# Unit 1 of the output projection in seven half-size products, with its weight sums earlier and batch 2's turns divided and moved

## The chip, the cores and the metric

One Trainium2 chip, one of its NeuronCores. The metric is the device time of one execution in microseconds (us). Five engines with a queue of instructions each work side by side: TensorE (PE in the profile; PEld is its weight load), VectorE (DVE), ScalarE (ACT), GpSimd (POOL) and SyncE (SP, which here only issues DMAs). They wait for each other through semaphores.

## The reference

Attention with a forget gate, then a two-layer network without a bias. With 8 batches, 8 heads, 576 positions and a head size of 64:

```python
scores = (q @ k.T) / 8 + cum[:, None] - cum[None, :]   # cum = cumsum(log(clip(f)))
scores = where(causal, -1e9, scores)
x = softmax(scores) @ v                                # 4608 tokens x 512, heads side by side
h = x @ w_in                                           # 512 -> 2048
g = h - tanh(h)
out = g @ w_out                                        # 2048 -> 512, float32
```

## The kernel before, in words

The attention is worked through in 32 **pairs** of heads, `(batch b, c)` with c from 0 to 3, and the network in nine **units** u of 512 tokens. The order on every engine is the order of the program text (a manual schedule), and the main loop is written as **slots** p = 4 to 32. Slot p (function `slot`, items from `att_items`) emits seven score tiles of pair p (`scores`, L342 on: matmuls L358 into two PSUM buffers, ScalarE's exponential L367, GpSimd's mask L377), the attention values of pair p-1 (`values`: 30 small matmuls L386, then three VectorE instructions L392 to L394 that divide by the row sum), and the turning of their result by two transposing DMAs on SP into the token ring XR (`turn`, L401 and L403). Between these items it emits steps of the network from one long list, `mlp`; `TAKE` says how many steps a slot takes, and they are spread evenly over the items that carry a name.

The network's first layer is `mlp1(u, s)`: four matmuls of 512 columns (L462; for unit 0 eight of 256, L448) into one of the three buffers of the PSUM pool `ps_m`, then `gate`: ScalarE's tanh (L414) and VectorE's sum of both (L415), which frees the buffer. The second layer has two forms.

- `mlp2(u, s)`, 16 steps for a unit: four matmuls of 512 columns each (L581), every fourth step an eviction by ScalarE (L585) and a store by SP (L587). Before the change units 0 and 1 use it.
- `seven(u, s)`, 14 steps for a unit: Strassen's scheme in Winograd's form, in which seven products of half size take the place of eight. Each step has eight matmuls of 256 columns (`product`, L503), into one running PSUM chain `cx` (from the one-buffer pool `ps_tr`) or a tile `cz` (from `ps_m`). ScalarE copies the chain out four times for a unit (`keep`, L540), VectorE adds four times (`add`, L496), SP stores four times (L493). It needs 16 sums of quarters of the unit's g (`sums`, L429, VectorE, 128x512), spread over the unit's steps by `mlp1` and `more_sums`. It also needs four sums of quarters of w_out, t1, t2, t3 and tn4, made once, in 16 VectorE instructions (`weight_sums`, L438). Units 2 to 8 use this form (`fast(u)`).

The weight sums lie in slots 11 to 14 (`LOADS`, L220). Of their results tn4 has a tile of its own; t1, t2 and t3 lie in the buffers `raw[0][1]` and `raw[1][1]`, which before that hold q and k of batch 1 and then of batch 3. Batch 3's are read out by one long transposing DMA for q (`turn_all` to TQ, slot 8) and one for k (to TK, slot 9), on SP.

For batches 1 and 2, q and k are turned by TensorE (`trans`, L245): six transposes (L254) into one PSUM tile, then two copies of 64x576 into QT or KT, one for the even and one for the odd columns (L260 to L266). Each copy is given to ScalarE (A, L261) or VectorE (V, L263) by a string of two letters: batch 1's q has "AV", batch 1's k and all of batch 2 have "VV". Slot p turns pair p+1: q at its score tile 0, k at tile 3 (in slot 7 at tiles 2 and 4). The PSUM tile comes from `ps_tr`, which has one buffer; k of batch 1 takes one from `ps_m`. Batch 2's q and k are loaded in slot 4 by GpSimd, in one DMA each (L214, L218).

Of the kernel before, what the change touches and what calls it, by code (L numbers as in the profile page):

```python
# [9 lines left out]
FP16 = mybir.dt.float16  # L10
# [7 lines left out]
FAR = 3  # L18
# [4 lines left out]
def kernel(  # L23
# [11 lines left out]
    P = 128  # L35

    B, H, S, D = q.shape
# [4 lines left out]
    NPAIR = H // 2  # L42
# [6 lines left out]
    NFT = DFF // P  # L49
# [3 lines left out]
    NU = NT // UW  # L53
# [3 lines left out]
    wpl = ctx.enter_context(tc.tile_pool(name="wpl", bufs=1))  # L57
# [11 lines left out]
    wout = wpl.tile([P, NFT, DM], FP16)  # L69
    HF, HD = NFT // 2, DM // 2  # L70
    SW = [wpl.tile([P, HF // 2, UW], FP16, tag=f"sw{i}", name=f"sw{i}") for i in range(2)]
    tn4 = wpl.tile([P, HF, HD], FP16, tag="tn4", name="tn4")
    RB = 3
    RING = RB * S
    XR = wpl.tile([P, NCH, RING], FP16)
# [5 lines left out]
    HP, LEAD = NJ * D, 2 * P  # L81
    TC = NPAIR * PITCH + LEAD
    TW = HF * HD
    tp = [raw[0][1][:, 0:TW], raw[1][1][:, 0:TW]]
    t2 = [raw[i][1][:, TW:TW + TW // 2].rearrange("p (k e) -> p k e", e=HD) for i in range(2)]
    t1, t3 = (x.rearrange("p (k e) -> p k e", e=HD) for x in tp)
    vn = [qkp.tile([P, NJ, H, VW], FP16, tag=f"vn{i}", name=f"vn{i}") for i in range(2)]
    QT = [qkp.tile([D + 3, H, S], FP16, tag=f"QT{i}", name=f"QT{i}") for i in range(2)]
    KT = [qkp.tile([D + 3, H, PITCH], FP16, tag=f"KT{i}", name=f"KT{i}") for i in range(2)]
# [12 lines left out]
    def load_heads(dst, src, b, n):  # L102
        pn = min(P, S - n * P)
        to = dst[0:pn, n * P:n * P + D]
        to = bass.AP(to.tensor, to.offset, [list(to.ap[0]), [HP, H], [1, D]])
        nc.gpsimd.dma_start(out=to, in_=src[b, :, n * P:n * P + pn, :].rearrange("h p d -> p h d"))  # L106

    def turn_all(dst, src):
        nc.sync.dma_start_transpose(out=dst.rearrange("p (x t) -> p x t", t=P), in_=src[:, 0:TC])
# [103 lines left out]
    def load_qk(dst, src, b, h0, h1):  # L213
        nc.gpsimd.dma_start(  # L214
            out=dst[b % 2][:, h0:h1, :, :].rearrange("p h n d -> p h (n d)"),
            in_=src[b, h0:h1, :, :].rearrange("h (p n) d -> p h (n d)", n=NT6))

    LOADS = {(NPAIR, 5): [lambda: load_qk(qn, q, 2, 0, H)],  # L218
             (NPAIR, 6): [lambda: load_qk(kn, k, 2, 0, H)]}
    for i in range(2 * HF):  # L220
        LOADS.setdefault((2 * NPAIR + 3 + i // 4, i % 4 * 2), []).append(lambda i=i: weight_sums(i))
    for b in range(2, B):
        p0 = (b - 1) * NPAIR
        for n in range(NJ):
            LOADS.setdefault((p0 + (2 if b == 2 else 1), n), []).append(lambda b=b, n=n: load_v(b, n))
        LOADS.setdefault((p0, 0), []).append(lambda b=b: load_aug(b))
        if b < FAR:
            continue
# [9 lines left out]
    E, XN, GT, M2, AV = {}, {}, {}, {}, {}  # L238
# [5 lines left out]

    def trans(b, c, src, dst, eng):  # L245
        pn, g3 = S // NT6, NT6 // 2
        if b == 1 and src is kn:
            t32 = ps_m.tile([P, UW], FP32, tag="m", name="t32")
        else:
            t32 = ps_tr.tile([P, UW], FP32, tag="tr", name="t32")  # L250
        t16 = t32.bitcast(FP16)[:, 0:2 * S // 2].rearrange("p (a g n) -> p a g n", a=2, g=g3)
        for a in range(2):
            for g in range(g3):
                nc.tensor.transpose(out=t16[:, a, g, :],  # L254
                                    in_=src[b % 2][:, 2 * c + a, 2 * g:2 * g + 2, :],
                                    identity=id16[0:pn, 0:pn])
        for e in range(2):
            to = dst[b % 2][0:D, 2 * c:2 * c + 2, e:S:2].rearrange("d a (p g) -> d a p g", g=g3)
            of = t16[e * D:(e + 1) * D, :, :, :].rearrange("d a g p -> d a p g")
            if eng[e] == "A":  # L260
                nc.scalar.activation(out=to, in_=of, func=AF.Copy)  # L261
            else:
                nc.vector.tensor_copy(out=to, in_=of)  # L263
# [134 lines left out]
    def turn(b, c):  # L398
        xn = XN.pop((b, c))
        r0 = b % RB * S  # L400
        nc.sync.dma_start_transpose(out=XR[:, c, r0:r0 + S - D].rearrange("p (n t) -> p n t", t=P),  # L401
                                    in_=xn[:, 0:NJ - 1, :].rearrange("p n d -> p (n d)"))
        nc.sync.dma_start_transpose(out=XR[:, c, r0 + S - D:r0 + S], in_=xn[D:P, NJ - 1, :])  # L403
# [11 lines left out]
        nc.vector.tensor_tensor(out=to, in0=view(hps), in1=view(th), op=ALU.add)  # L415

    def fast(u):
        return u > 1

    def quarter(u, k, hf, e):  # L420
        return G[(u, k)].rearrange("p (h e) n -> p h e n", h=2)[:, hf, e, :]
# [9 lines left out]
    def weight_sums(i):  # L431
        what, x = divmod(i, HF // 2)
        lo, hi = slice(2 * x, 2 * x + 2), slice(HF + 2 * x, HF + 2 * x + 2)
        b11, b12, b21, b22 = (wout[:, r, c] for r in (lo, hi) for c in (slice(0, HD), slice(HD, DM)))
        t2x = t2[x // 2][:, x % 2 * 2:x % 2 * 2 + 2, :]
        out, in0, in1 = ((t1[:, lo, :], b12, b11), (t2x, b22, t1[:, lo, :]),
                         (t3[:, lo, :], b22, b12), (tn4[:, lo, :], b21, t2x))[what]
        nc.vector.tensor_tensor(out=out, in0=in0, in1=in1, op=ALU.subtract)  # L438

    def mlp1(u, s):  # L440
# [43 lines left out]
    def moving(what, ft):  # L484
        if what[0] == "b":
            return wout[:, ft + HF * (what[1] == "2"), HD * (what[2] == "2"):HD * (what[2] == "2") + HD]
        if what == "t2":
            return t2[ft // 4][:, ft % 4, :]
        return {"t1": t1, "t3": t3, "tn4": tn4}[what][:, ft, :]
# [113 lines left out]

    FEW = {3: ("s1", "s4", "s6"), 4: ("s1", "s3", "s4", "s6")}

    def att_items(p):
# [3 lines left out]
        after = pairs[p + 1] if p + 1 < len(pairs) else None  # L610
        for ti in range(len(TILES)):
            if here:
                items.append((lambda ti=ti: scores(*here, ti), "s%d" % ti))
            for load in LOADS.get((p, ti), ()):
                items.append((load, ""))
            late = 2 * (p == 2 * NPAIR - 1)
            if ti == late and after and after[0] < FAR:
                items.append((lambda: trans(*after, qn, QT, "AV" if after[0] == 1 else "VV"), "q"))
            if ti == 1 and before:
                items.append((lambda: (values(*before), turn(*before)), "v"))  # L620
            if ti == 3 + late // 2 and after and after[0] < FAR:
                items.append((lambda: trans(*after, kn, KT, "VV"), "k"))
        return items

    goal = [0]
# [114 lines left out]
    scores0(4, 3)  # L740
    step()
    trans(1, 0, qn, QT, "AV")
    scores0(4, 4)
    turn0(3)
# [40 lines left out]
```

## Time and profile before

| | us |
|---|---|
| median of 3 runs | 345.33 (345.21 to 345.88) |
| the profiled execution | 346.0 |
| its span, first to last instruction | 344.3 |
| TensorE busy | 334.6 |
| VectorE busy | 236.2 |
| ScalarE busy | 222.9 |
| GpSimd busy | 158.6 |

The profile is of one execution; its own time is 0.67 us above the median and 1.7 us above its span. "Busy" on TensorE counts a matmul until its modelled end, so that it may be busy in the profile and still have waited; the way to find a wait is to lay out what a slot has to do and to compare that with the slot's length. A slot is counted here from the first of the 30 small matmuls of one pair's values (`av`) to the first of the next: slot 8's values begin at 65.58 us, slot 9's at 74.43, slot 10's at 85.33, slot 11's at 95.03.

### The profile page before, as it was taken

How to read it: one execution, taken by the hardware profiler on the slowest of the kernel's cores; microseconds unless marked ns; L12 is line 12 of the kernel's file. 1: busy time of each engine (PE TensorE's matmuls, PEld its weight loads, DVE VectorE, ACT ScalarE, POOL GpSimd, SP SyncE). 2: the span in 40 equal slices, each digit the busy share in tenths (PEclk: the TensorE clock that was granted, in tenths of full speed). 3: DMA queues.
4: the chain of work that ended last, by engine and by line, in shares of the span. 5: the costliest groups of instructions: out<-in, count | busy, mean ns of one | idle time of the engine just before them, and what ended most of it. 6: DMA issues, size and time to landing. Idle time of an engine off the chain costs nothing.

```text
span 344.3 us, 8688 instructions
## 1 busy us (share of the span) xinstructions
PE 334.6 (97%) x3354; PEld 235.2 (68%) x3354; DVE 236.2 (69%) x481; ACT 222.9 (65%) x417; POOL 158.6 (46%) x318
## 2 busy tenths in 40 slices
PE   7989999999999999999999999999999999999995
PEld 3879875655455557888886568656887786486485
DVE  6496886658953598558764895478637865975973
ACT  4677976558755786578757875687568844623631
POOL 8966448755267726664586548652222210000000
PEclk9999999999999999999999999999999999999999
DMA  9999999999799999999999999999330013002002
GB/s 88 140 197 188 204 203 141 169 159 233 126 141 127 202 175 151 123 193 184 164 145 188 172 159 181 182 172 184 91 110 19 17 50 109 3 30 93 0 32 91
DMA packets 161323, 45.96 MB, mean 134 GB/s; under 512 B 141506, under 2 KB 159234, under 8 KB 161282
## 3 DMA queue, kind: packets, MB, share of 16 engines
q0 software_dynamic: 100128, 18.36, 74.8%
q1 hardware_dynamic: 61074, 26.99, 39.8%
q8 instruction: 26, 0.43, 0.6%
q14 instruction: 15, 0.12, 0.1%
q10 hardware_dynamic: 80, 0.07, 0.1%
HBM read 36.85 MB, written 9.44 MB: 134 GB/s over the span
## 4 chain that ended last, share of the span: by engine, by line
PE 88%; DVE 5%; ACT 4%; POOL 1%; issue 1%; DMA 1%; ACTq 0%; DVEq 0%
PE hps L462 31%; PE cx L503 14%; PE cz L503 11%; PE ps L358 10%; PE ops L581 7%; PE av L386 7%; PE hps L448 2%; PE ps L300 2%; DVE gt L415 1%; PE t L272 1%; ACT e L305 1%; DVE QT L263 1%; ACT e L367 1%; ACT th L414 1%; PE av L313 1%
## 5 line engine op out<-in xcount | busy, mean ns | idle before, releaser
L415 DVE TENSOR_TENSOR gt<-hps,th 128x512 f16<-128x512 f32 x144 | 98.4, 688 | 42.7 <-ACT th L414 41.6
L462 PE MATMUL hps<-XR,win 128*128 128x512 f16 (+4 forms) x640 | 125.7, 336 | 0.2 <-DVE gt L415 0.2
L367 ACT ACTIVATE e<-ps 128x512 f16<-128x512 f32 x168 | 98.5, 594 | 37.4 <-PE ps L358 34.7
L414 ACT ACTIVATE th<-hps 128x512 f32<-128x512 f32 x144 | 86.1, 598 | 29.5 <-PE hps L462 19.8
L377 POOL TENSOR_SCALAR_AFFINE_SELECT e<-e 128x128 f16<-128x128 f16 x162 | 55.3, 342 | 105.9 <-ACT e L367 105.6
L462 PEld LDWEIGHTS <-win 128*128 128x128 f16 x640 | 56.3, 97 | 43.7 <-issue 0.5
L358 PE MATMUL ps<-QT,KT 67*128 67x512 f16 (+1 forms) x336 | 68.7, 277 | 0.5 <-DVE KT L263 0.3
L503 PEld LDWEIGHTS <-gt 128*128 128x128 f16 x560 | 52.5, 97 | 8.2 <-DVE gt L415 0.4
L358 PEld LDWEIGHTS <-KT 67*128 67x128 f16 x336 | 31.9, 98 | 21.7 <-DVE KT L263 0.8
L95 POOL DMA_DIRECT2D vn<-in_v_dram x40 | 34.2, 859 | 5.9 <-DMA win<-in_moe_w_in_dram 3.0
L581 PE MATMUL ops<-wout,gt 128*128 128x512 f16 x128 | 32.6, 378 | 0.0
L386 PEld LDWEIGHTS <-e 128*128 128x128 f16 x784 | 28.1, 97 | 3.3
L496 DVE TENSOR_TENSOR snap<-cz,snap 128x512 f32<-128x512 f32 x21 | 14.5, 691 | 22.4 <-PE cz L503 7.4
L386 PE MATMUL av<-vn,e 128*128 128x65 f16 x784 | 29.2, 193 | 0.0
L503 PE MATMUL cz<-wout,gt 128*128 128x256 f16 x224 | 27.8, 272 | 0.0
L394 DVE TENSOR_TENSOR xn<-av,rs 128x640 f16<-128x640 f32 x28 | 23.1, 825 | 1.0
L503 PEld LDWEIGHTS <-sw 128*128 128x128 f16 x224 | 21.1, 97 | 3.9
L106 POOL DMA_DIRECT2D qn<-in_q_dram x25 | 21.3, 852 | 1.7 <-issue 1.7
L106 POOL DMA_DIRECT2D kn<-in_k_dram x25 | 21.3, 853 | 1.2 <-issue 1.2
L540 ACT ACTIVATE snap<-cx 128x512 f32<-128x512 f32 (+1 forms) x16 | 8.7, 544 | 16.2 <-PE cx L503 16.2
L581 PEld LDWEIGHTS <-gt 128*128 128x128 f16 x128 | 11.2, 97 | 9.8
L305 ACT ACTIVATE e<-ps 128x512 f16<-128x512 f32 x25 | 14.3, 596 | 4.9 <-PE ps L303 2.9
(108 smaller groups left out, 377.4 us busy)
## 6 DMA issues: line engine op xcount, KB each, us to landing
vn<-in_v_dram POOLq DMA_DIRECT2D x32, 128.0 KB, 6.7
out_dram<-ost SPq DMA_DIRECT2D x14, 256.0 KB
out_dram<-snap SPq DMA_DIRECT2D x14, 256.0 KB
qn<-in_q_dram POOLq DMA_DIRECT2D x24, 128.0 KB, 5.3
kn<-in_k_dram POOLq DMA_DIRECT2D x24, 128.0 KB, 4.5
QT<-TQ SPq DMA_DIRECT2D x10, 288.0 KB
KT<-TK SPq DMA_DIRECT2D x10, 288.0 KB
win<-in_moe_w_in_dram POOLq DMA_DIRECT2D x2, 1024.0 KB, 12.1
```

What stands on the lines that cost most here:

```text
L95: nc.gpsimd.dma_start(out=dst[0:pn, n, h0:h1, 0:D], in_=src[b, h0:h1, n * P:n * P + pn, :].rearrange("h p d -> p h d"))
L106: nc.gpsimd.dma_start(out=to, in_=src[b, :, n * P:n * P + pn, :].rearrange("h p d -> p h d"))
L358: nc.tensor.matmul(out=ps[:, col:col + n], lhsT=KT[b % 2][0:D + 3, h, j * P:(j + 1) * P], rhs=QT[b % 2][0:D + 3, h, i0:i0 + n], start=True ...
L367: nc.scalar.activation(out=e[:, lo:hi], in_=ps[:, lo:hi], func=AF.Exp, scale=qscale)
L377: nc.gpsimd.affine_select(out=view, in_=view, compare_op=ALU.is_ge, fill=0.0, base=0, pattern=pat, channel_multiplier=-1)
L386: nc.tensor.matmul(out=av[:, a, ib, :], lhsT=E.pop((b, 2 * c + a, j, ib)), rhs=vn[b % 2][:, j, 2 * c + a, 0:D + 1], start=(j == 0), stop=( ...
L394: nc.vector.tensor_tensor(out=xn.rearrange("p i (a d) -> p a i d", a=2), in0=av[:, :, :, 0:D], in1=rs.to_broadcast([P, 2, NJ, D]), op=ALU. ...
L414: nc.scalar.activation(out=th, in_=hps, func=AF.Tanh, scale=-1.0)
L415: nc.vector.tensor_tensor(out=to, in0=view(hps), in1=view(th), op=ALU.add)
L462: nc.tensor.matmul(out=hps[:, o:o + n], lhsT=win[:, ci, ft * P:(ft + 1) * P], rhs=XR[:, ci, t:t + n], start=(ci == 0), stop=(ci == NCH - 1))
L503: nc.tensor.matmul(out=ps, lhsT=stationary(u, LHS[ph], ft, m), rhs=moving(RHS[ph], ft), start=fresh and ft == 0, stop=(ft == HF - 1), skip ...
L581: nc.tensor.matmul(out=ops, lhsT=GT[(u, ft, m)], rhs=wout[:, ft, :], start=(ft == 0), stop=(ft == NFT - 1))
```

## The change

Six edits.

- Unit 1 uses the seven products (`fast(u)` is `u > 0`), 14 steps in place of 16. `TAKE` is lowered by one in slots 13 and 15, so that from the end of slot 16 on the list stands where it stood.
- The weight sums move to slots 8 to 12, in the order t1, t2, t3, tn4.
- So that t1 can be made before batch 3's q and k have left their buffers, t1 gets the tile of its own, t2 and t3 a buffer each, and tn4 the rest of both.
- Batch 2's copies are "AV": the even columns by ScalarE, the odd ones by VectorE. In the program that results, VectorE's copy of each waits for ScalarE's copy of the same tile.
- Batch 2's turns: pair 0 in slot 7 and pair 1 in slot 8 as before; pair 2's q at slot 8's tile 5 and k at slot 9's tile 0 (before: slot 9, tiles 0 and 3); pair 3's q and k at slot 9's tiles 3 and 6 (before: slot 10, tiles 0 and 3). Pair 0's k takes its PSUM tile from `ps_m`.
- Batch 2's q and k are loaded in two halves each: heads 0 to 3 of q and of k, then heads 4 to 7.

```diff
-    tn4 = wpl.tile([P, HF, HD], FP16, tag="tn4", name="tn4")
+    t1 = wpl.tile([P, HF, HD], FP16, tag="t1", name="t1")
-    t2 = [raw[i][1][:, TW:TW + TW // 2].rearrange("p (k e) -> p k e", e=HD) for i in range(2)]
-    t1, t3 = (x.rearrange("p (k e) -> p k e", e=HD) for x in tp)
+    t2, t3 = (raw[i][1][:, 0:TW].rearrange("p (k e) -> p k e", e=HD) for i in range(2))
+    tn4 = [raw[i][1][:, TW:TW + TW // 2].rearrange("p (k e) -> p k e", e=HD) for i in range(2)]
-    LOADS = {(NPAIR, 5): [lambda: load_qk(qn, q, 2, 0, H)],
-             (NPAIR, 6): [lambda: load_qk(kn, k, 2, 0, H)]}
-    for i in range(2 * HF):
-        LOADS.setdefault((2 * NPAIR + 3 + i // 4, i % 4 * 2), []).append(lambda i=i: weight_sums(i))
+    LOADS = {(NPAIR, 5): [lambda: load_qk(qn, q, 2, 0, HH), lambda: load_qk(kn, k, 2, 0, HH)],
+             (NPAIR, 6): [lambda: load_qk(qn, q, 2, HH, H), lambda: load_qk(kn, k, 2, HH, H)]}
+    q0 = 2 * NPAIR
+    for i, at in enumerate(((q0, 1), (q0, 3), (q0, 5), (q0 + 1, 1),
+                            (q0 + 1, 5), (q0 + 2, 1), (q0 + 2, 3), (q0 + 2, 5),
+                            (q0 + 3, 1), (q0 + 3, 3), (q0 + 3, 5), (q0 + 3, 6),
+                            (q0 + 4, 0), (q0 + 4, 1), (q0 + 4, 2), (q0 + 4, 3))):
+        LOADS.setdefault(at, []).append(lambda i=i: weight_sums(i))
...
-        if b == 1 and src is kn:
+        if src is kn and (b, c) <= (2, 0):
...
-        return u > 1
+        return u > 0
...
-    mlp += [(fn, 1, s) for fn in (mlp1, mlp2) for s in range(NFT)]
-    mlp += [(fn, u, s) for u in range(2, NU) for fn, n in ((mlp1, NFT), (seven, 14)) for s in range(n)]
+    mlp += [(fn, u, s) for u in range(1, NU) for fn, n in ((mlp1, NFT), (seven, 14)) for s in range(n)]
...
+    for b, c, at_q, at_k in [(1, c, (NPAIR + c - 1, 0), (NPAIR + c - 1, 3)) for c in range(1, NPAIR)] + [
+            (2, 0, (q0 - 1, 2), (q0 - 1, 4)), (2, 1, (q0, 0), (q0, 3)),
+            (2, 2, (q0, 5), (q0 + 1, 0)), (2, 3, (q0 + 1, 3), (q0 + 1, 6))]:
+        TRANS.setdefault(at_q, []).append(((b, c), qn, QT, "AV"))
+        TRANS.setdefault(at_k, []).append(((b, c), kn, KT, "VV" if b == 1 else "AV"))
...
-    TAKE = [4, 4, 5, 5, 7, 9] + 7 * [8] + 4 * [8, 7, 8, 7]
+    TAKE = [4, 4, 5, 5, 7, 9] + [8, 8, 8, 7, 8, 7, 8] + 4 * [8, 7, 8, 7]
```

More of the change, by code (lines that the diff above doesn't have):

```diff
@@ L83 @@
     TW = HF * HD
-    tp = [raw[0][1][:, 0:TW], raw[1][1][:, 0:TW]]
-    t2 = [raw[i][1][:, TW:TW + TW // 2].rearrange("p (k e) -> p k e", e=HD) for i in range(2)]
-    t1, t3 = (x.rearrange("p (k e) -> p k e", e=HD) for x in tp)
+    t2, t3 = (raw[i][1][:, 0:TW].rearrange("p (k e) -> p k e", e=HD) for i in range(2))
+    tn4 = [raw[i][1][:, TW:TW + TW // 2].rearrange("p (k e) -> p k e", e=HD) for i in range(2)]
     vn = [qkp.tile([P, NJ, H, VW], FP16, tag=f"vn{i}", name=f"vn{i}") for i in range(2)]
@@ L434, in weight_sums @@
         b11, b12, b21, b22 = (wout[:, r, c] for r in (lo, hi) for c in (slice(0, HD), slice(HD, DM)))
-        t2x = t2[x // 2][:, x % 2 * 2:x % 2 * 2 + 2, :]
-        out, in0, in1 = ((t1[:, lo, :], b12, b11), (t2x, b22, t1[:, lo, :]),
-                         (t3[:, lo, :], b22, b12), (tn4[:, lo, :], b21, t2x))[what]
+        tn4x = tn4[x // 2][:, x % 2 * 2:x % 2 * 2 + 2, :]
+        out, in0, in1 = ((t1[:, lo, :], b12, b11), (t2[:, lo, :], b22, t1[:, lo, :]),
+                         (t3[:, lo, :], b22, b12), (tn4x, b21, t2[:, lo, :]))[what]
         nc.vector.tensor_tensor(out=out, in0=in0, in1=in1, op=ALU.subtract)
@@ L486, in moving @@
             return wout[:, ft + HF * (what[1] == "2"), HD * (what[2] == "2"):HD * (what[2] == "2") + HD]
-        if what == "t2":
-            return t2[ft // 4][:, ft % 4, :]
-        return {"t1": t1, "t3": t3, "tn4": tn4}[what][:, ft, :]
+        if what == "tn4":
+            return tn4[ft // 4][:, ft % 4, :]
+        return {"t1": t1, "t2": t2, "t3": t3}[what][:, ft, :]
     def store(u, e, d, src, m0=0, m1=2):
@@ L604 @@
     FEW = {3: ("s1", "s4", "s6"), 4: ("s1", "s3", "s4", "s6")}
+    TRANS = {}
+    for b, c, at_q, at_k in [(1, c, (NPAIR + c - 1, 0), (NPAIR + c - 1, 3)) for c in range(1, NPAIR)] + [
[3 more added lines that the diff above has]
+        TRANS.setdefault(at_k, []).append(((b, c), kn, KT, "VV" if b == 1 else "AV"))
     def att_items(p):
@@ L609, in att_items @@
         before = pairs[p - 1] if NPAIR < p else None
-        after = pairs[p + 1] if p + 1 < len(pairs) else None
         for ti in range(len(TILES)):
@@ L615, in att_items @@
                 items.append((load, ""))
-            late = 2 * (p == 2 * NPAIR - 1)
-            if ti == late and after and after[0] < FAR:
-                items.append((lambda: trans(*after, qn, QT, "AV" if after[0] == 1 else "VV"), "q"))
             if ti == 1 and before:
                 items.append((lambda: (values(*before), turn(*before)), "v"))
-            if ti == 3 + late // 2 and after and after[0] < FAR:
-                items.append((lambda: trans(*after, kn, KT, "VV"), "k"))
+            for pair, src, dst, engs in TRANS.get((p, ti), ()):
+                items.append((lambda pair=pair, src=src, dst=dst, engs=engs: trans(*pair, src, dst, engs),
+                              "q" if dst is QT else "k"))
         return items
```

## The prediction

> **What bounds the kernel now.** I read the page first: the busy shares, the granted clock, and the chain of waits.
>
> ```profile
> span 344.3 us, 8688 instructions
> PE 334.6 (97%) x3354; PEld 235.2 (68%) x3354; DVE 236.2 (69%) x481; ACT 222.9 (65%) x417; POOL 158.6 (46%) x318
> PEclk9999999999999999999999999999999999999999
> PE 88%; DVE 5%; ACT 4%; POOL 1%; issue 1%; DMA 1%; ACTq 0%; DVEq 0%
> ```
>
> TensorE is the bound, at a full clock throughout, and 88% of the chain is its own work. So an instruction less on TensorE is worth its full time wherever TensorE is dense, and the 9% of the chain on VectorE and ScalarE are waits that might go. Where they lie I read from a view by stretches, one stretch for each slot from the first `av` matmul to the next (slots 7, 8, 9, 10, 12, 14 and 15; columns: length, then busy time and count of each engine):
>
> ```profile
> core 0: us, PE busy (x) PEld busy (x) DVE busy (x) ACT busy (x) POOL busy (x), PEclk, DMA share, GB/s
> 56.32:65.58 9.26, 8.45 (x94) 5.58 (x92) 7.20 (x11) 5.34 (x11) 7.40 (x14) 1.00 2.69 152
> 65.58:74.43 8.85, 8.85 (x84) 5.00 (x82) 5.01 (x8) 5.14 (x10) 5.92 (x12) 1.00 2.27 158
> 74.43:85.33 10.90, 10.75 (x92) 5.79 (x91) 7.68 (x13) 7.56 (x15) 5.98 (x12) 1.00 1.61 216
> 85.33:95.03 9.70, 9.61 (x81) 5.14 (x80) 8.71 (x15) 7.80 (x16) 2.82 (x8) 1.00 0.80 140
> 104.24:113.44 9.20, 9.20 (x76) 4.88 (x75) 2.85 (x7) 4.95 (x9) 6.44 (x13) 1.00 1.36 146
> 122.64:131.84 9.20, 9.20 (x75) 4.87 (x74) 9.11 (x20) 7.87 (x16) 2.29 (x7) 1.00 1.04 162
> 131.84:141.13 9.29, 9.29 (x108) 8.02 (x107) 6.25 (x15) 5.63 (x11) 7.01 (x13) 1.00 1.87 165
> ```
>
> The fifth row is a slot with eight `mlp2` steps and no wait. The chain of waits gives the parts of a slot:
>
> ```profile
> 100.28 0.86 PE ops L581 x4
> 101.36 0.87 PE ops L581 x4
> 88.40 0.26 PE t L254 x6
> 134.01 0.88 PE cx L503 x8
> 95.19 0.91 PE av L386 x30
> ```
>
> Four matmuls of 512 columns take 0.865 us, so that slot is 8 x 0.865 = 6.92 and 2.28 of attention (0.91 of values and seven score tiles of 0.2). From that each earlier slot can be laid out. Slot 7's stretch has four such steps, two of eight matmuls (0.875) and three turns (0.26): 3.46 + 1.75 + 2.28 + 0.78 = 8.27, against 9.26: 0.99 waited. Slot 8: 7 x 0.865 + 2.28 + 0.52 = 8.86 against 8.85: nothing. Slot 9: 9 x 0.865 + 2.28 + 0.52 = 10.59 against 10.90: 0.31. Slot 10: 6.92 + 2.28 + 0.26 = 9.46 against 9.70: 0.24. Together 1.54 us. The timeline says who made TensorE wait (brackets: idle before, and the releaser):
>
> ```profile
> 53.34 1.60 DVE L263 COPY KT<-t 64x576 f16<-64x576 f16 x2
> 57.15 0.69 DVE L415 TENSOR_TENSOR gt<-hps,th 128x512 f16<-128x512 f32 x1 [2.21 <-ACT th L414]
> 58.94 1.60 DVE L263 COPY QT<-t 64x576 f16<-64x576 f16 x2
> 60.69 0.42 PE L254 MATMUL t<-id,kn 96*128 96x96 f16 x6 [0.81 <-DVE QT L263]
> 79.65 1.61 DVE L263 COPY KT<-t 64x576 f16<-64x576 f16 x2
> 82.04 1.02 PE L462 MATMUL hps<-XR,win 128*128 128x512 f16 x4 [0.15 <-DVE gt L415]
> 89.61 1.61 DVE L263 COPY KT<-t 64x576 f16<-64x576 f16 x2
> ```
>
> It is VectorE's pairs of copies, 1.6 us long (the first two rows are used below): in slot 7 k's turn waits for the one `ps_tr` buffer, in slots 9 and 10 the gates queue behind them and a `ps_m` buffer comes free late.
>
> **The seven products.** The cleanest price is in the tail, where nothing else runs on TensorE:
>
> ```profile
> 288.45 13.81 PE hps L462 x64
> 302.26 1.85 PE cx L503 x16
> 314.59 13.81 PE hps L462 x64
> ```
>
> 64 matmuls of 512 columns, as many as `mlp2` has for a unit, take 13.81 us. The 112 of 256 columns between take 314.59 - 302.26 = 12.33. Slots agree: eight seven-steps take 9.29 (last stretch), eight `mlp2` steps 9.20. So unit 1 saves 13.81 - 12.33 = **1.5 us** of TensorE, in slots 11 to 13, which are dense. The Trainium skill speaks against it (TensorE: Matmul & The Clock Gate, section "Back-to-back issue gap": a sustained stream of loads and matmuls at about 131 ns for 512 columns and 81 for 128). By an estimate of mine from it, about 98 ns for 256 columns, the change would lose 112 x 98 - 64 x 131 ns = 2.6 us; the tail's 216 and 110 ns disagree, and the measurement decides.
>
> Beside it lie 16 sums and four adds of unit 1 on VectorE; ScalarE's four evictions become four copies of the chain, SP's four stores four others of as many bytes. Their cover is below.
>
> **The turns of batch 2.** Eight times two copies on VectorE become eight on each engine. They aren't in parallel: VectorE's waits for ScalarE's. Batch 1's q shows what that does:
>
> ```profile
> 48.67 0.83 ACT L261 ACTIVATE QT<-t 64x576 f16<-64x576 f16 x1
> 49.54 0.80 DVE L263 COPY QT<-t 64x576 f16<-64x576 f16 x1 [0.48 <-ACT QT L261]
> ```
>
> From the first to the last 1.67 us, no shorter than VectorE's pair. Queued behind VectorE's waiting copy are gates, weight sums and the division L392 to L394; for the gates TensorE waits (through `ps_m`), for the division the transposing DMAs. What is won is VectorE's time (8 x 0.8) and not latency, so I went through the queues by hand, with the durations above.
>
> Slot 7: k takes a `ps_m` buffer that was last read at 53.34 + 1.60 = 54.9, so its turn need not wait for q's copies and starts at 59.7, when the score tile ahead of it is done, in place of 60.69; the next `mlp1` follows at 60.0, its buffer free since 57.15 + 0.69 = 57.8. This 0.95 us is kept up to slot 8's values. There unit 0's last `mlp1` step now follows the values, and takes the buffer that ScalarE evicts at 64.3 in my count, before 64.7 when it is wanted. Slot 8: three turns in the one `ps_tr` buffer with two steps and two score tiles, 2 x 0.865 + 2 x 0.2 = 2.1 us, between two; the copies need 0.2 to start, in my count up to 0.2 more behind an exponential, 0.83 and 0.8: just enough, 0.1 to spare at the last. Slot 9: three of VectorE's copies in place of four, two weight sums and two sums more; the gates end 0.3 us or more before their buffers are wanted. Slot 10: no copies. In my count slot 11's values end 1.3 us earlier than in the profile. Of the 1.54 that leaves 0.25 waited: **1.3 us**. From below: nothing, if the serial copies cost what the pairs did; from above all 1.54.
>
> **VectorE with the sums.** Prices, from the view of a line's instructions (minimum/median/maximum in ns):
>
> ```profile
> L438 DVE TENSOR_TENSOR qn<-wout x4: 414/537/646, 95.4 to 98.6; 128x512 f16<-128x512 f16 x4
> L438 DVE TENSOR_TENSOR tn<-wout,qn x2: 407/408/410, 123.3 to 127.3; 128x512 f16<-128x512 f16 x2
> L429 DVE TENSOR_TENSOR sw<-gt x28: 414/424/599, 120.8 to 329.8; 128x512 f16<-128x512 f16 x28
> ```
>
> The fullest is slot 10: eight gates, the division, four sums, three weight sums. Slot 14 before (122.64) has eight gates, the division, four sums and four weight sums: VectorE 9.11 of 9.20, and TensorE loses nothing. So slot 10 costs **nothing** where it begins without a backlog; I count 0.9 us of backlog against three `ps_m` buffers, just covered. Slots 11 and 12 are like slots 15 and 16 (6.25 of 9.29 in the last row) with four weight sums each, 1.7 us: covered. The weight sums taken out of slots 13 and 14 gain nothing there, since TensorE didn't wait.
>
> **SP, GpSimd and the transfers.**
>
> ```profile
> 71.11 4.16 SPq L109 DMA_TRANSPOSE TQ<-qn  x1
> 85.19 1.41 SPq L113 DMA_DIRECT2D QT<-TQ  x2
> 143.97 1.24 SPq L401 DMA_TRANSPOSE XR<-xn  x1
> 148.44 1.04 PE L462 MATMUL hps<-XR,win 128*128 128x192 f16 x8
> 37.80 0.77 POOL L214 DMA_DIRECT2D kn<-in_k_dram  x1
> 41.83 0.29 POOL L377 TENSOR_SCALAR_AFFINE_SELECT e<-e 128x128 f16<-128x128 f16 x1 [3.25 <-ACT e L367]
> ```
>
> The first t2 sum (slot 9, tile 5) overwrites what TQ's transposing DMA reads. That is issued until 75.3 and has landed before its reader at 85.19; the sum comes at about 81.5. I take it as landed: unit 3's turn below, issued until 145.2, has landed by 148.44, 3.2 us later, and 75.3 + 3.2 = 78.5. At worst VectorE stands until 85.2. Unit 2 now starts right after slot 12's pair has been turned, ahead of slot 13's values: that is how unit 3 stands before the change, its turn issued at 143.97, its matmul at 148.44 without a wait. A weight sum ahead of the division makes xn 0.4 us later: covered. The two additional loads take 2 x 0.77 of GpSimd, which idles 3.25 us there: nothing.
>
> **Sum.** 1.5 + 1.3 = 2.8 us. The profiled execution, 346.0 with 1.7 around its span, would be 343.2; it lies 0.67 above the median of the runs, so the forecast is 345.33 - 2.8 = **342.5 us**.
>
> **The rivals.**
> - *The copies gain nothing.* ACT then DVE takes as long as the pair (1.67 against 1.6), which speaks for it; against it that the 0.81 in slot 7 was a buffer, and that one is now avoided. Only the products are left: 343.8.
> - *VectorE becomes the bound in slots 9 to 11.* 8.7 us of work in slot 10 (slot 14's 9.11 less one weight sum) in 9.2, with a backlog. If each of the nine sums and weight sums of slot 10 and its neighbourhood takes the maximum of the rows, 0.6 in place of 0.42, that is 1.6 us which TensorE waits: 345.33 - 2.8 + 1.6 = 344.1. The Trainium skill names a mechanism (SBUF — State Buffer, section "Who interferes with whom"): a VectorE instruction with two inputs in SBUF contends with a GpSimd instruction that reads SBUF, and whoever comes second waits. The spread of 414 to 646 ns would fit. Against it: slot 14 had the same mix.
> - *Slower: the serial copies hold up the gates.* In slot 9 a tanh waits 0.7 behind ScalarE's copy, its gate 0.8 behind VectorE's and up to 0.8 more while VectorE waits: with the tanh's own 0.6 and the gate's 0.7 that is 0.7 + 0.6 + 1.6 + 0.7 = 3.6 us, where three buffers cover two steps and their score tiles, about 2.4. That is 1.2 for each of the two turns there, and 0.35 for each of two in slot 8 if an exponential (0.6) always stands ahead of ScalarE's copy: 3.1 us on top of the old 1.54. It gives 345.33 - 1.5 + 3.1 = 346.9. It is slower from the point where the new waits exceed the 1.5 of the products. For it, VectorE's wait of 0.48 above; against it, that ScalarE is 69% busy in slot 9 (7.56 of 10.90).
> - *The products cost more than they save.* Each half-size matmul has a weight load of its own:
>
> ```profile
> L503 PEld LDWEIGHTS <-gt 128*128 128x128 f16 x560 | 52.5, 97 | 8.2 <-DVE gt L415 0.4
> ```
>
> If a third of unit 1's 112 loads were not hidden, 37 x 97 ns = 3.6 us, the products would lose 2.1, and with the copies' 1.3 it would be 346.1. The rule of that page of the Trainium skill would point this way; 110 ns for each matmul in the tail leave no room for it.
> - *TQ lands late.* VectorE stands 85.2 - 81.5 = 3.7 us, TensorE, after what its buffers cover, some 2.5: 345.0.
>
> **How the numbers follow.** Forecast 0.62; copies gain nothing 0.16; VectorE the bound 0.12; serial copies 0.06; products cost more 0.01; late TQ 0.03. A measurement tells 0.2% (0.7 us) from no change. Faster by more: the forecast and the first two rivals, 0.90, less 0.05 of VectorE's case, which may take more than I allow: 0.85. Slower: serial copies and the dearer products, 0.07. Same: the late TQ and the 0.05, 0.08. The range reaches from the full 1.54 and 1.57 (342.2) with half a microsecond for what the stretches don't show, 341.7, to VectorE's case and a little more, 344.2; what is left out is 0.10 of the rivals beyond and some of VectorE's, with room for what I overlooked.
>
> **What would show it.** Slot 7's stretch shorter by 0.9, with `t<-id,kn` no longer released by DVE QT. Slot 9 and 10 without DVE gt as a releaser of `hps`. L503 with 112 matmuls more, L581 with 64 fewer, and 1.5 us between slot 11 and slot 14. VectorE near full in slot 10. Wrong would be: `hps` or `t` waiting for L261 or L263 in slots 8 and 9, VectorE waiting for a DMA at the first t2 sum, or a wait of `hps` on XR at unit 2's start.

## The result, and the profile after

The kernel takes **343.19 us** after the change (median of four executions, 343.03 to 343.36), before it 345.33 (345.21 to 345.88). The two medians differ by 2.1 us; the ratio of times on record, with a 95% interval, is 0.9926 [0.9907, 0.9945], which is 2.6 us (1.9 to 3.2). The forecast was 342.5, the range 341.7 to 344.2. In a later comparison of the same two kernels the ratio was 0.9911 [0.9878, 0.9945].

The page of the changed kernel: span, busy shares, and the chain of waits.

```profile
span 341.7 us, 8813 instructions
PE 333.2 (98%) x3402; PEld 240.5 (70%) x3402; DVE 237.9 (70%) x493; ACT 227.2 (66%) x425; POOL 160.6 (47%) x320
PE 91%; DVE 4%; ACT 3%; DMA 1%; issue 0%; ACTq 0%; DVEq 0%
```

The span is 2.6 us shorter. TensorE's own work is 91% of the chain in place of 88, while VectorE, ScalarE and GpSimd have gone from 10 to 7. TensorE has more instructions and less busy time, as half-size products should. Where the time came from shows in the view by stretches, again from one slot's first `av` matmul to the next; these are slots 7 to 15 of the changed kernel:

```profile
core 0: us, PE busy (x) PEld busy (x) DVE busy (x) ACT busy (x) POOL busy (x), PEclk, DMA share, GB/s
56.72:64.20 7.48, 7.48 (x87) 4.86 (x84) 4.12 (x7) 6.11 (x12) 6.63 (x14) 1.00 2.75 160
64.20:74.19 9.99, 9.99 (x98) 6.04 (x97) 6.03 (x11) 7.98 (x15) 7.11 (x13) 1.00 2.49 155
74.19:84.78 10.59, 10.59 (x92) 5.79 (x91) 7.95 (x15) 8.57 (x17) 5.89 (x12) 1.00 2.17 201
84.78:93.97 9.19, 9.19 (x75) 4.87 (x74) 8.94 (x21) 7.86 (x16) 2.97 (x8) 1.00 1.16 179
93.97:103.26 9.29, 9.29 (x108) 8.01 (x107) 8.32 (x20) 5.64 (x11) 6.62 (x13) 1.00 1.20 121
103.26:111.65 8.39, 8.39 (x97) 6.84 (x94) 4.91 (x11) 4.26 (x9) 5.52 (x11) 1.00 1.24 103
111.65:120.85 9.20, 9.20 (x75) 4.88 (x74) 6.93 (x13) 8.04 (x16) 6.73 (x13) 1.00 1.59 200
120.85:129.21 8.36, 8.36 (x71) 4.49 (x70) 7.47 (x15) 7.03 (x15) 1.99 (x6) 1.00 1.34 212
129.21:138.50 9.29, 9.29 (x108) 8.01 (x107) 5.85 (x14) 5.51 (x11) 7.27 (x14) 1.00 1.38 131
```

In every row TensorE is busy for the whole stretch. The same nine slots took 141.13 - 56.32 = 84.81 us before and take 138.50 - 56.72 = 81.78 now: **3.03 us** less. The profiled execution reached slot 7 0.40 us later than that of before (a matter of the executions, see the last section), which leaves 2.63, the difference of the spans. So all of the gain lies in these slots.

It has two parts. Slots 7 to 10, the turns' part: 38.71 before, 37.25 now, 1.46 less with the same eight turns in them. (One step of eight matmuls, 0.875 us, moved from slot 7's stretch to slot 8's, and one turn from slot 10's to slot 8's, so the two kernels can't be compared slot by slot without laying out.) Slots 11 to 15, the products' part: 141.13 - 95.03 = 46.10 before, 138.50 - 93.97 = 44.53 now, 1.57 less.

### The profile page after: what moved, and what is told of

Read it like the earlier page. It is cut to its first block, busy times and chain, and to the rows that moved or that the text cites. A ratio compares the mean times of both kernels' runs of the same rounds, so it can differ in the third digit from the quotient of the medians.

```text
span 341.7 us, 8813 instructions
## 1 busy us (share of the span) xinstructions
PE 333.2 (98%) x3402; PEld 240.5 (70%) x3402; DVE 237.9 (70%) x493; ACT 227.2 (66%) x425; POOL 160.6 (47%) x320
## 4 chain that ended last, share of the span: by engine, by line
PE 91%; DVE 4%; ACT 3%; DMA 1%; issue 0%; ACTq 0%; DVEq 0%
PE hps L465 32%; PE cx L506 16%; PE cz L506 12%; PE ps L361 11%; PE av L389 7%; PE ops L584 4%; PE hps L451 3%; PE ps L303 2%; PE t L275 1%; ACT e L308 1%; DMA snap<-in_f_dram 1%; DVE gt L418 1%; PE t L257 1%; PE av L316 1%; DVE KT L266 1%; PE ps L306 1%
## 5 line engine op out<-in xcount | busy, mean ns | idle before, releaser
L380 POOL TENSOR_SCALAR_AFFINE_SELECT e<-e 128x128 f16<-128x128 f16 x162 | 56.0, 346 | 102.0 <-ACT e L370 101.6
L506 PEld LDWEIGHTS <-gt 128*128 128x128 f16 x640 | 59.9, 97 | 9.5 <-DVE gt L418 0.4
L499 DVE TENSOR_TENSOR snap<-cz,snap 128x512 f32<-128x512 f32 x24 | 16.6, 691 | 23.3 <-ACT e L370 10.1
L506 PE MATMUL cz<-wout,gt 128*128 128x256 f16 x256 | 32.0, 272 | 0.0
L506 PEld LDWEIGHTS <-sw 128*128 128x128 f16 x256 | 24.0, 97 | 4.5
L506 PE MATMUL cx<-kn,gt 128*128 128x256 f16 x192 | 25.7, 272 | 0.0
L543 ACT ACTIVATE snap<-cx 128x512 f32<-128x512 f32 (+1 forms) x18 | 9.9, 549 | 16.7 <-PE cx L506 16.7
L451 PE MATMUL hps<-XR,win 128*128 128x256 f16 x128 | 16.6, 272 | 0.3 <-DVE gt L418 0.3
```

What stands on the lines that cost most here:

```text
L380: nc.gpsimd.affine_select(out=view, in_=view, compare_op=ALU.is_ge, fill=0.0, base=0, pattern=pat, channel_multiplier=-1)
L451: nc.tensor.matmul(out=hps[:, w * SB:(w + 1) * SB], lhsT=win[:, ci, ft * P:(ft + 1) * P], rhs=XR[:, ci, t * SB:(t + 1) * SB], start=(ci == ...
L506: nc.tensor.matmul(out=ps, lhsT=stationary(u, LHS[ph], ft, m), rhs=moving(RHS[ph], ft), start=fresh and ft == 0, stop=(ft == HF - 1), skip ...
```

## The experiments

Times of single executions of one kernel spread over 2 to 5 us here (before 344.04 to 347.05, e3 343.25 to 348.38), so beside the times I give the stretches of the profiled execution: from slot 7's first `av` matmul, us, sums of slots as in the section above. Stretches of the same instructions mostly agree within 0.05 us between executions. Of e5 to e11 there is one execution each: 343.50, 346.32, 346.83, 344.24, 344.80, 346.42 and 342.99 us in the order of their numbers, beside single ones of before of 345.86 (e5 to e8) and 345.12 (e9 to e11). Given the spread these times decide nothing; the stretches do.

| kernel | slots 7+8 | 9 | 10 | 11 | 12 | 13 to 15 | 7 to 15 | against before |
|---|---|---|---|---|---|---|---|---|
| before | 18.11 | 10.90 | 9.70 | 9.21 | 9.20 | 27.69 | 84.81 | |
| after | 17.47 | 10.59 | 9.19 | 9.29 | 8.39 | 26.85 | 81.78 | -3.03 |
| after, again | 17.47 | 10.58 | 9.20 | 9.28 | 8.40 | 26.84 | 81.77 | -3.04 |
| e1, products only | 18.12 | 10.89 | 11.76 | 9.28 | 8.39 | 26.85 | 85.29 | +0.48 |
| e2, turns only | 17.46 | 10.59 | 9.20 | 9.20 | 9.20 | 27.69 | 83.34 | -1.47 |
| e3, one engine | 17.60 | 10.82 | 9.82 | 9.28 | 8.39 | 26.85 | 82.76 | -2.05 |
| e9, old places | 17.20 | 10.58 | 10.36 | 9.28 | 8.40 | 26.84 | 82.66 | -2.15 |
| e7, sums twice | 17.61 | 10.58 | 9.98 | 9.28 | 12.17 | 26.85 | 86.47 | +1.66 |

With the old places a turn (0.26 us of TensorE) lies in slot 10 that the new places put into slot 8, so between kernels with different places the sum counts.

**e4, the changed kernel again**, as the foot of the scale, with no edit.

> The changed kernel once more, unchanged, for more runs and a second trace. Theory (the first 14 us differ from execution to execution with the moment at which TensorE comes to full speed): the stretches from slot 7 on repeat within 0.05 us, the start of slot 7's values moves by some tenths of a us against 56.72, and the time lies 2.1 to 3.0 below before. Rival (the change itself makes the start 0.4 later): 56.72 again within 0.05.

342.23 us against 345.87 for before (29 executions, 344.04 to 347.05), the ratio given above, -3.1 us (-1.9 to -4.2). The stretches are those of after to 0.02 us.

**e1, the products alone.** Unit 1 in seven products with the early sums, while batch 2's copies, places, PSUM tile and loads stay as before. The edit is against after; its lines for the loads and the PSUM tile are left out here.

```diff
...
-            (2, 2, (q0, 5), (q0 + 1, 0)), (2, 3, (q0 + 1, 3), (q0 + 1, 6))]:
+            (2, 2, (q0 + 1, 0), (q0 + 1, 3)), (2, 3, (q0 + 2, 0), (q0 + 2, 3))]:
-        TRANS.setdefault(at_q, []).append(((b, c), qn, QT, "AV"))
-        TRANS.setdefault(at_k, []).append(((b, c), kn, KT, "VV" if b == 1 else "AV"))
+        TRANS.setdefault(at_q, []).append(((b, c), qn, QT, "AV" if b == 1 else "VV"))
+        TRANS.setdefault(at_k, []).append(((b, c), kn, KT, "VV"))
```

> The seven products of unit 1 with the early weight sums and the new buffers for them, but batch 2's turns as before (both copies on VectorE, before's places, whole loads, one PSUM buffer). Theory (the turns' edits pay for VectorE's room): slot 10 then holds eight gates, the division, four copies, four sums and three weight sums, about 4.9 + 1.2 + 3.2 + 1.7 + 1.2 = 12.2 us of VectorE where TensorE has 9.5, so slots 9 and 10 together grow by 2 to 3 us, the products take 1.5 off, and the kernel ends 0.5 to 1.5 us above before. Rival (the parts are independent): the stretches of slots 7 to 10 stay at 9.26, 8.85, 10.90 and 9.70, and the kernel ends 1.5 us below before.

Slower than before: 1.0028 [1.0006, 1.005], and the stretches have +0.48. Slots 11 to 15 have the whole gain of the products (1.57), and slot 10 gives it back and more. Its stretch and the one before it:

```profile
core 0: us, PE busy (x) PEld busy (x) DVE busy (x) ACT busy (x) POOL busy (x), PEclk, DMA share, GB/s
74.71:85.60 10.89, 10.74 (x92) 5.79 (x91) 8.17 (x16) 7.56 (x15) 5.97 (x12) 1.00 1.61 202
85.60:97.36 11.76, 9.93 (x82) 5.15 (x81) 11.48 (x22) 7.68 (x16) 3.03 (x8) 1.00 0.88 139
```

VectorE is busy 11.48 of 11.76 us, TensorE 9.93: in this slot VectorE is the bound. The timeline of the same kernel shows how it gets to TensorE:

```profile
91.95 1.60 DVE L266 COPY KT<-t 64x576 f16<-64x576 f16 x2
93.58 2.10 DVE L418 TENSOR_TENSOR gt<-hps,th 128x512 f16<-128x512 f32 x3
94.33 1.02 PE L465 MATMUL hps<-XR,win 128*128 128x512 f16 x4 [1.52 <-DVE gt L418]
```

Behind the pair of copies three gates have queued up, all three `ps_m` buffers are taken, and the next `mlp1` step waits 1.52 us for the first of them. So the products with their sums (four of unit 1's g and three weight sums in slot 10) cost 2.06 us there, where VectorE still has the copies of batch 2.

**e2, the turns alone**: places, division, PSUM tile and loads as after, unit 1 with `mlp2`, the weight sums in their old slots. Of the edit against after one line is shown; the list `mlp`, `TAKE` and the slots of the weight sums go back with it.

```diff
...
-        return u > 0
+        return u > 1
...
```

> The divided and moved turns, the other PSUM buffer and the halved loads, with unit 1 in its 16 steps of mlp2, the weight sums in slots 11 to 14 and before's TAKE. Theory: the waits of slots 7 to 10 go as in the changed kernel, 1.4 us below before, stretches of 7.5, 10.0, 10.6 and 9.2 or a little less. Rival (the gain of the trace comes from the products alone, the waits only move): within 0.3 us of before.

0.9958 [0.9938, 0.9978], -1.5 us (-0.8 to -2.1); the stretches have -1.47, all of it in slots 7 to 10. With the turns' edits the products are worth 83.34 - 81.78 = 1.56; without them they cost 0.48. The two parts are not independent: the turns' edits make the room on VectorE that the sums need.

**e3, one engine for each copy pair, in the new places.** Batch 2's copies are "VV" again, all else as after.

```diff
-        TRANS.setdefault(at_q, []).append(((b, c), qn, QT, "AV"))
-        TRANS.setdefault(at_k, []).append(((b, c), kn, KT, "VV" if b == 1 else "AV"))
+        TRANS.setdefault(at_q, []).append(((b, c), qn, QT, "AV" if b == 1 else "VV"))
+        TRANS.setdefault(at_k, []).append(((b, c), kn, KT, "VV"))
```

> The changed kernel with both copies of batch 2's turns on VectorE again, in the new places. Theory (the division is what makes room): slot 9 has 6 copies of 0.8 beside 6 gates, the division, two sums and two weight sums, 11.4 us of VectorE for 10.6 of TensorE, so slots 8 to 10 grow by 0.8 to 1.5 us and the kernel ends 0.8 to 1.5 above the changed one. Rival (the new places and the other PSUM buffer alone remove the waits): within 0.2 of the changed kernel, stretches 7.5, 10.0, 10.6 and 9.2.

0.9968 [0.9941, 0.9996]; the stretches give up 0.98 of the gain, in slots 7 to 10 (0.13, 0.23 and 0.63). The largest is slot 10, although its copies now lie ahead of it. The last pair, in VectorE's timeline:

```profile
83.79 1.61 DVE L266 COPY KT<-t 64x576 f16<-64x576 f16 x2
85.44 0.69 DVE L418 TENSOR_TENSOR gt<-hps,th 128x512 f16<-128x512 f32 x1
```

It ends at 85.40, slot 10 begins at 85.21, and VectorE starts the fullest slot with gates queued.

**e9, divided copies in the old places.** All as after, except for the places of the last two pairs.

```diff
-            (2, 2, (q0, 5), (q0 + 1, 0)), (2, 3, (q0 + 1, 3), (q0 + 1, 6))]:
+            (2, 2, (q0 + 1, 0), (q0 + 1, 3)), (2, 3, (q0 + 2, 0), (q0 + 2, 3))]:
```

> The changed kernel with batch 2's turns in before's places (pair 2 in slot 9, pair 3 in slot 10), the copies divided. Theory (division and places are both needed, as VectorE's room in slot 10 decides): slot 10 holds two copies of 0.8 beside eight gates, the division of the rows, four sums and three weight sums, 10.6 us of VectorE for 9.5 of TensorE's work, so slots 9 and 10 together (20.6 of TensorE's work less the places' 0.5, which go from slot 8 to them) take 0.5 to 1.2 us more than laid out, and from slot 7's values to slot 16's it is 82.2 to 83.0 in place of 81.78. Rival (the division alone suffices): 81.8 within 0.1.

82.66 for the nine slots, +0.88 on after. The wait is where it was in "products only", smaller by half; the timeline of this kernel, in slot 10:

```profile
91.65 1.02 PE L465 MATMUL hps<-XR,win 128*128 128x512 f16 x4 [0.74 <-DVE gt L418]
```

So division and places each take about 0.9 to 1.0 us out, and both are needed. In slot 10 of this kernel VectorE is busy 10.07 of 10.36 us, which fits VectorE's work up to and in slot 10 as what decides.

**e5, the buffer alone**: the kernel before, with one word changed, so that k of pair (2, 0) takes its PSUM tile from `ps_m`.

```diff
-        if b == 1 and src is kn:
+        if src is kn and (b, c) <= (2, 0):
```

> Before with one edit: pair 0 of batch 2 turns its k into a buffer of ps_m. Theory (a wait is removed, but the next one is close): k's turn no longer waits 0.81 us, but the last mlp1 step of unit 0, which stands ahead of slot 8's values here, gets the buffer that ScalarE has just evicted, and waits some 0.5 us; slot 7's stretch falls from 9.26 to 8.8 to 9.0, the others stay. Rival (the buffer is all there is to it): slot 7 falls to 8.3 to 8.4.

Slot 7's stretch is 8.36 in place of 9.26, and no other slot gives any of it back: -0.90. The turn of k and the `mlp1` step at which I had expected a new wait, in the timeline of this kernel:

```profile
58.10 0.42 PE L254 MATMUL t<-id,kn 96*128 96x96 f16 x6
62.19 1.04 PE L448 MATMUL hps<-XR,win 128*128 128x256 f16 x8
```

Neither has a bracket, so neither waited. My 0.5 us of a follow-on wait did not come; the rival holds. Of the 1.47 of the turns' edits the buffer is 0.90, and the rest, 0.57, is the division and the places together.

**e6, whole loads**: after, with batch 2's q and k in one DMA each again.

```diff
-    LOADS = {(NPAIR, 5): [lambda: load_qk(qn, q, 2, 0, HH), lambda: load_qk(kn, k, 2, 0, HH)],
-             (NPAIR, 6): [lambda: load_qk(qn, q, 2, HH, H), lambda: load_qk(kn, k, 2, HH, H)]}
+    LOADS = {(NPAIR, 5): [lambda: load_qk(qn, q, 2, 0, H)],
+             (NPAIR, 6): [lambda: load_qk(kn, k, 2, 0, H)]}
```

> The changed kernel with batch 2's q and k loaded in one DMA each, as before. Theory (the halves gain nothing): all stretches from slot 7 on as in the changed kernel, 7.48, 9.99, 10.59, 9.19, within 0.05. Rival (pair 0's k, turned 0.6 to 0.9 us earlier now, would wait for a whole load, which landed at 37.8 + 20.6 = 58.4 in before): slot 7's stretch 7.6 to 8.5.

The stretches of slots 7 to 14 are those of after to 0.02 us, slot 15 has 9.41 in place of 9.29. The halves bring nothing that shows. But this execution reached slot 7 only at 59.55 us, in place of 56.72 (why, is told in the last section), so a late load could hardly show in it. The harder case is e5, with whole loads too and slot 7 at 54.70: its turn of k at 58.10, shown above, did not wait either. An early execution of after with whole loads was not seen.

**e7, every weight sum twice**, to see how much room VectorE has left.

```diff
         nc.vector.tensor_tensor(out=out, in0=in0, in1=in1, op=ALU.subtract)
+        nc.vector.tensor_tensor(out=out, in0=in0, in1=in1, op=ALU.subtract)
```

> The changed kernel with each of the 16 weight sums made twice (the second writes the same values again). Theory (VectorE is full in slot 10, with 0.25 us to spare): slots 9 to 11 get 2, 3 and 4 sums of 0.42 more, the stretch of slot 10 grows by 0.8 to 1.5 us and those of slots 8, 9 and 12 by less than 0.2. Rival (VectorE still has room there): every stretch within 0.2 of the changed kernel.

Slot 10 grows by 0.79 us, with VectorE busy 9.81 of 9.98, and slot 8 by 0.14. Added were one sum late in slot 9 and three in slot 10, 4 x 0.41 = 1.6 us; TensorE feels half of it, so by this estimate after has some 0.8 us to spare there, where 0.25 was expected. Slot 12 was not expected: 12.17 in place of 8.39. In this kernel's timeline the products wait there for the sums of tn4:

```profile
109.88 0.38 PE L507 MATMUL cx<-kn,gt 128*128 128x256 f16 x2 [1.26 <-DVE kn L442]
110.67 0.38 PE L507 MATMUL cx<-kn,gt 128*128 128x256 f16 x2 [0.41 <-DVE kn L442]
```

That is 1.67 of the 3.78. Most of the rest is seen in the view by stretches of the same kernel, in the column PEclk:

```profile
108.00:111.00 3.00, 1.33 (x11) 0.89 (x10) 2.93 (x7) 0.60 (x1) 1.51 (x4) 1.00 1.66 118
111.00:114.40 3.40, 3.40 (x16) 1.91 (x14) 0.22 (x1) 1.92 (x4) 0.58 (x2) 0.51 0.90 207
```

After a stretch in which TensorE was busy 1.33 of 3.00 us, the granted clock was 0.51 for 3.4 us, which is another 1.7 us of work not done. So a wait of TensorE can cost more than its length. This came once; behind e1's single wait of 1.52 us the clock stayed at 1.00, and where the limit lies was not tested.

Three tries at what is left, the waits in slots 5 and 6 (laid out like the others they need 7.17 and 6.89 us and take 7.62 and 7.33):

**e8, batch 1's k divided too.**

```diff
-        TRANS.setdefault(at_k, []).append(((b, c), kn, KT, "VV" if b == 1 else "AV"))
+        TRANS.setdefault(at_k, []).append(((b, c), kn, KT, "AV"))
```

> The changed kernel with batch 1's k divided between ScalarE and VectorE too. Laid out like slot 7, the stretches of slots 5 and 6 hold 7.17 and 6.89 us of TensorE's work and take 7.62 and 7.33, so 0.9 us is waited, and VectorE's pair of copies of k (1.6 us) is in both chains. Theory (it is these copies that hold up the gates): slots 5 and 6 fall together by 0.3 to 0.9. Rival (ScalarE, with two of its copies in a slot, takes over): within 0.2 of 7.62 and 7.33 together, or longer.

Slots 5 and 6 take 7.59 and 7.29, no gain to speak of, as the rival said. ScalarE has taken VectorE's place; the chain of waits of this kernel, in slot 6:

```profile
52.62 0.60 ACT th L417
53.22 0.69 ACT KT L264
53.91 0.45 ACT e L370
```

**e10, a whole pair of copies to each engine**: q's to ScalarE, k's to VectorE, for batches 1 and 2, so that neither waits for the other.

```diff
-        TRANS.setdefault(at_q, []).append(((b, c), qn, QT, "AV"))
-        TRANS.setdefault(at_k, []).append(((b, c), kn, KT, "VV" if b == 1 else "AV"))
+        TRANS.setdefault(at_q, []).append(((b, c), qn, QT, "AA"))
+        TRANS.setdefault(at_k, []).append(((b, c), kn, KT, "VV"))
```

> The changed kernel with q's two copies both on ScalarE and k's both on VectorE, for batches 1 and 2, so that neither engine waits for the other's copy. Theory (VectorE's wait for ScalarE's copy costs nothing in slots 7 to 10, since no wait of TensorE is left there): slots 7 to 11 give 46.5 us within 0.2 or more, no gain; slots 5 and 6 (7.62 and 7.33 with 7.17 and 6.89 of work) fall by 0.2 to 0.6, since VectorE no longer waits for q's first copy there. Rival (the waiting copies still cost time): slots 7 to 11 fall by more than 0.2.

No gain in slots 7 to 11, but 2.09 us worse, which neither theory had: 48.63 us in place of 46.54, with slots 8, 9 and 10 all longer. Slot 5 rose to 8.14 from 7.62 where a fall was expected, and slot 6 stayed at 7.33. Where slot 9 goes over into slot 10 (at 86.71), its chain of waits has the pair of copies in one piece again, with a gate behind it:

```profile
85.91 0.71 DVE KT L266
86.64 0.81 DVE KT L266
87.47 0.69 DVE gt L418
```

The wait within a divided pair is thus cheaper than it looks. In slot 9 of after's timeline, VectorE runs a gate while ScalarE copies the even columns, and waits little or not at all for its own copies:

```profile
77.88 0.69 DVE L418 TENSOR_TENSOR gt<-hps,th 128x512 f16<-128x512 f32 x1 [1.30 <-ACT th L417]
77.90 0.81 ACT L264 ACTIVATE QT<-t 64x576 f16<-64x576 f16 x1
78.74 0.81 DVE L266 COPY QT<-t 64x576 f16<-64x576 f16 x1 [0.18 <-ACT QT L264]
83.40 0.80 DVE L266 COPY KT<-t 64x576 f16<-64x576 f16 x1
```

**e11, batch 1's q on VectorE**, the opposite direction.

```diff
-        TRANS.setdefault(at_q, []).append(((b, c), qn, QT, "AV"))
+        TRANS.setdefault(at_q, []).append(((b, c), qn, QT, "VV" if b == 1 else "AV"))
```

> The changed kernel with both copies of batch 1's q on VectorE. Theory (in slots 5 and 6 it is the length of the chain ScalarE's copy, VectorE's copy, division, gate that TensorE waits for): VectorE idles 0.45 us ahead of its copy today, and starts both earlier, so slots 5 and 6 fall together by 0.2 to 0.5. Rival (ScalarE or GpSimd bounds these slots): within 0.1 of 7.62 and 7.33.

Slot 5 takes 7.95 in place of 7.62 and slot 6 7.33 as before, where a fall was expected, so this is no way either. What was not expected is in slot 10, 9.76 in place of 9.19, though the edit is far from it. VectorE's first t2 sum, in the timeline:

```profile
80.64 0.42 DVE L441 TENSOR_TENSOR qn<-wout,t 128x512 f16<-128x512 f16 x1 [0.79 <-DMA TQ<-qn]
87.26 1.02 PE L465 MATMUL hps<-XR,win 128*128 128x512 f16 x4 [0.40 <-DVE gt L418]
```

The sum waited 0.79 us for batch 3's q to be read out by the transposing DMA, and in slot 10 TensorE waited for a gate. The chain of this execution puts the DMA down with

```profile
69.08 11.44 DMA TQ<-qn
```

from the start of its issue to its landing at 80.52. This looks like the late TQ of the prediction, at a small price. It need not come from the edit: this execution reached slot 7 at 54.65 us, 2.07 us earlier than that of after, while TQ's issue began only 0.62 us earlier (69.08 against 69.70), so the transfer is late against the slots. No version came out that beats after by more than 0.1 us of these stretches; what holds slots 5 and 6 up stays open.

## Why the prediction was right, point by point

- **The seven products.** Forecast 1.48, measured 1.57 in slots 11 to 15 of after, and 1.58 in e1, e3 and e4. The tail's 110 and 216 ns for a matmul hold in the middle of the kernel. The rival of the dearer products falls with it.
- **The turns.** Forecast 1.3 of the 1.54 waited, measured 1.46: 0.25 was to be left, and 0.08 is. Slot 7 alone was forecast at 0.95 and gave 0.90 (e5), with the cause that was named: the turn of k has no releaser any more.

```profile
60.11 0.42 PE L257 MATMUL t<-id,kn 96*128 96x96 f16 x6
71.13 0.81 DVE L266 COPY QT<-t 64x576 f16<-64x576 f16 x1 [1.60 <-ACT QT L264]
73.55 0.80 DVE L266 COPY KT<-t 64x576 f16<-64x576 f16 x1 [1.62 <-ACT KT L264]
71.99 0.42 PE L257 MATMUL t<-id,kn 96*128 96x96 f16 x6
```

  These are rows of after. In slot 8 the copy of q ends at 71.13 + 0.81 = 71.94 and the turn of k, which wants the same PSUM buffer, begins at 71.99 without a wait: "just enough", as counted. The brackets show VectorE idle 1.60 and 1.62 us behind ScalarE's copies. I feared that idleness for the gates (the slower rival), but it costs TensorE nothing here, and in slot 9, where that rival put most of its price, VectorE waited 0.18 us for q's copy and not at all for k's (rows at e10). Slots 7 to 10, laid out like the others, need 7.40, 9.99, 10.59 and 9.20 and take 7.48, 9.99, 10.59 and 9.19.
- **VectorE with the sums: nothing.** Right for this kernel (8.94 of 9.19 in slot 10, TensorE without a wait), but by less than a microsecond of room (e7), and only since the other edits made it. The prediction added the two parts up, and its rival "the copies gain nothing" priced the products alone at a gain of 1.5, as if they needed nothing of the turns; without the turns' edits they lose 0.48 (e1). A full VectorE, another of its rivals, is what they meet without the turns' edits, at 2.06 us. But it comes of copies ahead of the gates, not of slower sums, so that 2.06 is near the 1.6 I gave it is luck.
- **TQ landed in time: right, narrowly and by luck.** In after the first t2 sum came at 81.84 without a wait, as this row of its timeline shows. The estimate behind it was wrong: from the start of the issue I counted 7.4 us to the landing (71.11 to 78.5), with the time that unit 3's turn took; in e11 it took 11.44, which is 4 us more. In after it took at most 12.1 (69.70 to 81.84), so the error was not punished.

```profile
81.84 0.60 DVE L441 TENSOR_TENSOR qn<-wout,t 128x512 f16<-128x512 f16 x1
110.78 1.03 PE L465 MATMUL hps<-XR,win 128*128 128x512 f16 x4
```

- **Unit 2's start and the loads: nothing.** Right. Unit 2's first matmul (the second row) has no wait on XR, and whole loads give the same stretches (e6).
- **The rival "the copies gain nothing"** falls with e2, in which the turns' edits alone gain 1.47, and with e3 and e9: undoing the division costs 0.98, undoing the places 0.88.
- **The sum.** By the stretches it is 3.03 against the forecast 2.8; the ratios of the times say 2.6 (1.9 to 3.2) in the first comparison and 3.1 (1.9 to 4.2) in the second. The loose step is the reference: the prediction took a median as good to 0.2%, while executions of one program differ by 2 to 5 us, mostly for a reason that has nothing to do with the change (last section). The forecast came out between the two medians of after, 342.23 and 343.19.

## What to carry to other kernels

Work that is added to an engine off the critical path is free only up to the room in the fullest stretch: count that room there, and make it first, or the gain of one edit pays for another (products alone +0.48, with the turns' edits -1.56). Dividing a pair of copies between two engines can pay though it shortens nothing, because it takes work off the engine on which the gates queue. Where times of single executions scatter more than the effect, compare stretches of the traces between two fixed instructions.

## What the runs showed of the hardware

**When TensorE gets its full speed differs between executions.** The groups of four early 128-column transposes show it. Timeline of before:

```profile
11.69 0.63 PE L272 MATMUL t<-id,kn 128*67 128x128 f16 x4
13.41 0.39 PE L272 MATMUL t<-id,qn 128*67 128x128 f16 x4
```

of after:

```profile
13.63 0.61 PE L275 MATMUL t<-id,qn 128*67 128x128 f16 x4
14.06 0.40 PE L275 MATMUL t<-id,kn 128*67 128x128 f16 x4
```

of e4, the same program as after:

```profile
6.20 0.41 PE L275 MATMUL t<-id,qn 128*67 128x128 f16 x4 [0.29 <-DVE qn L198]
9.48 0.63 PE L275 MATMUL t<-id,qn 128*67 128x128 f16 x4
12.41 0.38 PE L275 MATMUL t<-id,qn 128*67 128x128 f16 x4
```

and of e6:

```profile
20.81 0.63 PE L275 MATMUL t<-id,kn 128*67 128x128 f16 x4
```

Four take 0.63 us at first and 0.38 to 0.41 later. The step comes at about 13.0 us in before, 14.1 in after, 5.1 in e4 (which falls back for a while) and 21.6 in e6, and slot 7 is reached at 56.32, 56.72, 55.33 and 59.55. What follows slot 15 then takes 203.1 us to the end of the span in all four. So the start, 4.2 us between e4 and e6, is large enough for most of the scatter between executions of one kernel (before: 344.04 to 347.05), though only the profiled executions show it. There is a smaller source later: in e8, e9 and e11 one slot somewhere behind slot 15 is 0.7 to 1.2 us longer, where TensorE waits for a transfer, into XR in e8 and e9 and from TK in e11. The profile's granted clock says 1.00 in the early stretches of before, after and e6, and the prediction read "a full clock throughout" from it. But the clock's record in each of these traces begins only at the step, and the view counts what lies before as 1.00; the spacing of equal matmuls is the better witness. In e4 the record begins early, and the view does say 0.50 between 8.49 and 11.90:

```profile
8.49:11.90 3.41, 3.23 (x33) 2.95 (x31) 0.69 (x3) 1.83 (x4) 3.41 (x5) 0.50 2.18 139
```

The Trainium skill (TensorE: Matmul & The Clock Gate, section "What's actually happening") tells of a gate that grants half the clock until a free-running window of about 3.4 us has been busy, so that the moment varies between executions. The 3.41 us of this row and the 3.40 of e7's agree with it; the page's spread of about half a microsecond in either direction does not, against 5.1 to 21.6 us here.

**Two-input sums slow down beside GpSimd's masks.** In after, of its 144 fp16 sums of 128x512 on VectorE, the 56 with no GpSimd instruction beside them take 0.41 to 0.43 us; of the 75 that overlap a mask, 37 take more than 0.45 and the longest 0.65. That agrees with the Trainium skill (SBUF — State Buffer, section "Who interferes with whom"), by which GpSimd and a VectorE instruction with two SBUF inputs contend. In slots 7 to 15 of after TensorE is busy throughout all the same.

**A divided pair of copies does not run side by side in this program**, although the engines write different columns: VectorE's copy begins only after ScalarE's of the same tile, with waits of 1.60, 1.62 and 0.18 us in the rows above. These are waits for a semaphore of the program; whether the engines could copy at the same time, or independent tiles would lift the wait, was not tried.
